# Attention and MLP in one kernel: a new order for the first loads, group sums on TensorE for two batches, and an earlier table load

## The chip, the cores and the metric

One core of a Trainium2 chip runs the whole kernel. The metric is the device time in microseconds (us). Each kernel is run several times, in rounds together with the kernel before on the same chip, and one run is recorded by the hardware profiler. Every run has a state, fast or slow, as judged by its time against the fastest run of the same kernel. A median that is quoted is of all runs.

Terms used throughout: TensorE (PE in the profile) multiplies matrices; PEld is its weight load; DVE is VectorE, ACT is ScalarE, POOL is GpSimd, SP issues transfers. A batch is one of the 8 attention batches. A group is 512 tokens of the MLP: nine groups, 0 to 8. "mm1" is the first MLP matmul of a group with its silu, "mm2" is the second. In the program, the attention of batch g+1 is interleaved with mm2 of group g.

## The reference, cut to what matters

```python
def _attn_ref(q, k, v):                   # q, k, v: [8, 8, 576, 64] float32
    q_d, k_d, v_d = mean of 4 neighbouring rows of q, k, v      # 144 rows
    out_d = softmax(q_d k_d^T / 8) v_d                          # coarse attention
    out_up = np.repeat(out_d, 4, axis=2)
    # local attention: only keys with |i - j| < 4
    out_local = softmax(masked q k^T / 8) v
    return out_up + out_local
# then x = the result as [4608, 512];  h = x @ w_in [512, 2048]
# g = h * sigmoid(1.702 h);  out = g @ w_out [2048, 512]
```

## The kernel before: the parts that matter

The prologue loads q/k, v and the weights, and computes attention of batch 0. v is loaded twice: once as rows for the local part (`load_v`, cast by `prep_v` to `vb`), once with four rows side by side (`load_v4`), from which `prep_v4` adds up the four-row sums (`vd`).

```python
    for qd in range(NQ):
        load_qk(0, qd)                     # gpsimd queue
    constants()                            # masks, identity, ones columns
    prep_qk(0, 0); pool_qk(0, 0)           # DVE transposes, POOL sums of four
    load_v(0, gate=lambda t: nc.vector.memset(t, 0.0))   # SP queue, 10 transfers
    load_v4(0)                                           # SP queue, 6 transfers
    load_w_in(0)
    prep_qk(0, 1); pool_qk(0, 1)
    # ... rest of w_in, q/k of batch 1, w_out
    steps = attention(0)
    # ... scores; prep_v(0), prep_v4(0) on DVE; load_v(1), load_v4(1); value part
    for g in range(n_groups):
        b = g + 1
        if b < B:
            # ... loads of q/k for b+1; transposes and sums for b;
            #     v and four-row v of b+1 cast and summed, those of b+2 loaded
        gT = mm1(g)
        steps = dict(zip(POS, attention(b))) if b < B else {}   # POS = [0, 18, 25, 32, 43, 52]
        mm2(g, gT, steps)                  # steps[n]() runs before matmul n of 64
```

The six steps of `attention` are: scores of the first half, scores of the second half, value part of two head pairs, of two more, transposes of two, of two more. They are hundreds of tiny matmuls:

```python
    def av(b, hp):                         # value part of one head pair: 44 matmuls
        o = ps_tile("av")
        for i in range(5):
            for par in range(2):
                for j in range(2):
                    # ...
                    nc.tensor.matmul(o[...], lhsT=E[...], rhs=vb[...], ...)     # es
        # ... 24 more for the coarse part, lhsT=Ed[...] (ed)
```

At the end of mm2 the table of ScalarE is switched back to silu:

```python
            nc.scalar.activation(out=osb, in_=ops, func=AF.Copy, scale=1.0 / GELU_SCALE)
            # ... store osb
        nc.scalar.preload_act_table_set("silu_and_others")
```

The softmax here doesn't subtract the row's maximum and nothing guards it: scores larger than these inputs give would overflow.

## Time and profile before

The median was 382.2 us (381.81 to 382.93, three runs). The profiled run has a span of 381.2 us.

The page cuts the span in 40 slices; each digit is the busy share in tenths, PEclk the clock granted to TensorE.

```profile
PE   0200369397799889988978899799999998999995
PEclk9999999789999999999999999999999999999999
DMA  7999999999769314961595149410010011002002
```

TensorE starves in the first five slices and is busy after that. The DMA engines are full while it starves (digits 7 to 9).

The chain of waits (start, length, what) gives the reason at the start:

```profile
8.54 0.73 SPq L129
...
17.57 11.85 DMA vf<-in_v_dram
29.60 1.51 DVE vb_86 L200
```

v of batch 0 is issued from 8.5 us and lands at 29.4 us. The four-row sums end later still, at 43.4 us, and steady mm1 matmuls run only from 53.9 us.

The windows view gives busy times by stage. I cut it at the first mm1 weight load of each group. The columns are the stretch, its length, busy time and number of instructions for each engine, the mean granted clock, the DMA share and the GB/s.

```profile
core 0: us, PE busy (x) PEld busy (x) DVE busy (x) ACT busy (x) POOL busy (x), PEclk, DMA share, GB/s
52.10:98.90 46.80, 36.12 (x620) 18.01 (x624) 18.72 (x27) 21.05 (x32) 26.34 (x26) 0.93 1.10 196
98.90:139.00 40.10, 35.09 (x618) 17.47 (x624) 14.22 (x25) 20.80 (x32) 17.34 (x19) 0.96 0.63 139
139.00:175.60 36.60, 33.47 (x619) 17.26 (x625) 15.02 (x26) 20.79 (x32) 17.34 (x19) 1.00 0.59 131
175.60:213.60 38.00, 33.25 (x619) 17.10 (x625) 14.96 (x26) 20.90 (x32) 17.34 (x19) 1.00 0.60 126
213.60:249.80 36.20, 32.94 (x618) 16.97 (x624) 14.88 (x25) 20.79 (x32) 17.35 (x19) 1.00 0.57 133
249.80:284.40 34.60, 32.84 (x618) 16.93 (x624) 14.87 (x25) 20.79 (x32) 15.23 (x15) 1.00 0.09 33
```

Rows are groups 0 to 5. Group 0 is stretched by waits for batch 1's data. Groups 1 to 4 take 36.2 to 40.1 us; group 5 takes 34.6 us.

A group boundary, ScalarE's timeline and the TensorE matmul that follows (start, length, engine, line, what; in brackets the idle time before it and what ended it):

```profile
139.43 0.60 ACT L445 ACTIVATE osb<-ops 128x512 f32<-128x512 f32 x1 [1.66 <-PE ops L438]
140.05 1.28 ACT L450 ACT_TABLE_LOAD   x1
141.34 1.09 ACT L424 ACTIVATE gT<-hps 128x512 bf16<-128x512 f32 x2
...
141.99 0.38 PE L418 MATMUL hps<-xT_82,w_in_bf 128*128 128x512 bf16 x1 [0.87 <-ACT gT L424]
```

The table load (1.28 us, begun 20 ns after the copy ends) stands between the last output copy and the first silu, and TensorE waits 0.87 us for that silu at each of the eight boundaries.

And a piece of the weight-load timeline in group 2:

```profile
163.33 1.19 PEld L438 LDWEIGHTS <-gT 128*128 128x128 bf16 x7
164.94 0.11 PEld L280 LDWEIGHTS <-es_92 64*64 64x64 bf16 x4 [0.42 <-DVE rc L306]
166.53 0.21 PEld L280 LDWEIGHTS <-es_92 64*64 64x64 bf16 x16 [1.48 <-issue]
```

TensorE stops after 4 of 20 weight loads of one tile, for 1.48 us, and the profile names no releaser ("issue").

### The profile page before, as it was taken

What the parts mean: (1) busy time and instruction counts of PE and PEld (TensorE: products, weight loads), DVE (VectorE), ACT (ScalarE), POOL (GpSimd) and SP (SyncE); (2) the same over time, 40 slices, a digit from 0 to 9 for tenths busy, and PEclk for the clock granted to TensorE, in tenths of its full rate; (3) what the DMA queues carried; (4) which work ended last, traced back from release to release, by engine and by line L of the source; (5) the groups of instructions that cost most, each with busy time, mean ns of one, the idle gap of its engine ahead of it and who ended that gap; (6) DMA issues with size and microseconds to landing.
All of it is one profiled execution on the core that took longest, in us unless ns stands there. A gap on an engine that the chain in (4) does not pass through costs nothing.

```text
span 381.2 us, 11310 instructions
## 1 busy us (share of the span) xinstructions
PE 302.0 (79%) x5065; PEld 153.9 (40%) x5120; DVE 133.2 (35%) x213; ACT 181.4 (48%) x278; POOL 140.8 (37%) x166
## 2 busy tenths in 40 slices
PE   0200369397799889988978899799999998999995
PEld 0200234244344444544444445444544454444442
DVE  6602681226600670157015702660473063000000
ACT  1400056432466266726661666267547726624622
POOL 7932004894593029504940494069007000000000
PEclk9999999789999999999999999999999999999999
DMA  7999999999769314961595149410010011002002
GB/s 124 176 199 237 209 210 189 187 186 189 204 147 197 103 56 91 215 142 55 122 195 132 57 107 223 125 51 2 31 58 28 3 58 57 0 29 83 0 29 83
DMA packets 66289, 43.73 MB, mean 115 GB/s; under 512 B 44224, under 2 KB 57536, under 8 KB 66240
## 3 DMA queue, kind: packets, MB, share of 16 engines
q1 hardware_dynamic: 57408, 29.37, 34.3%
q0 software_dynamic: 8832, 13.63, 20.0%
q8 instruction: 40, 0.66, 0.7%
q14 instruction: 9, 0.07, 0.1%
HBM read 47.19 MB, written 9.44 MB: 149 GB/s over the span
## 4 chain that ended last, share of the span: by engine, by line
PE 64%; SPq 11%; DMA 11%; ACT 5%; issue 5%; POOL 3%; DVE 1%; ACTq 0%; DVEq 0%; POOLq 0%
PE ops L438 29%; PE hps L418 26%; SPq L129 11%; DMA vf<-in_v_dram 5%; DMA out_dram<-osb 3%; ACT L450 3%; DMA v_96<-in_v_dram 2%; PE sd L243 2%; PE av L280 2%; PE av L294 1%; PE xt L322 1%; ACT osb L445 1%; DMA qb_101<-in_q_dram 1%; ACT gT L424 1%; POOL vb_86 L200 1%
## 5 line engine op out<-in xcount | busy, mean ns | idle before, releaser
L438 PE MATMUL ops<-w_out_bf,gT 128*128 128x512 bf16 x532 | 125.2, 382 | 6.8 <-issue 6.3
L424 ACT ACTIVATE gT<-hps 128x512 bf16<-128x512 f32 x144 | 85.1, 597 | 39.2 <-PE hps L418 39.1
L418 PEld LDWEIGHTS <-w_in_bf 128*128 128x128 bf16 x576 | 56.8, 99 | 80.3 <-issue 15.3
L438 PEld LDWEIGHTS <-gT 128*128 128x128 bf16 x576 | 53.2, 98 | 62.7 <-issue 3.4
L418 PE MATMUL hps<-xT_82,w_in_bf 128*128 128x512 bf16 x143 | 54.9, 384 | 8.2 <-ACT gT L424 7.0
L418 PE MATMUL hps<-xT_85,w_in_bf 128*128 128x512 bf16 x144 | 55.2, 383 | 0.9 <-DVE xT_85 L366 0.4
L418 PE MATMUL hps<-xT_83,w_in_bf 128*128 128x512 bf16 x143 | 55.2, 386 | 0.3 <-issue 0.3
L445 ACT ACTIVATE osb<-ops 128x512 f32<-128x512 f32 x36 | 21.5, 597 | 69.7 <-PE ops L438 48.0
L418 PE MATMUL hps<-xT_84,w_in_bf 128*128 128x512 bf16 x135 | 52.0, 385 | 0.1
L344 ACT COPY od<-xt 128x576 f32<-128x576 f32 x32 | 19.1, 642 | 63.9 <-PE xt L333 63.0
L268 DVE TENSOR_TENSOR es_90<-es_90,mask 128x600 bf16<-128x600 bf16 x8 | 6.7, 842 | 96.4 <-ACT es_90 L254 96.4
L308 DVE TENSOR_TENSOR y<-av,rc 128x896 bf16<-128x896 f32 x32 | 34.9, 1092 | 1.1
L200 POOL CAST vb_87<-vf 128x2560 bf16<-128x2560 f32 x4 | 9.3, 2321 | 23.8 <-DMA v_96<-in_v_dram 23.8
L268 DVE TENSOR_TENSOR es_92<-es_92,mask 128x600 bf16<-128x600 bf16 x8 | 4.7, 589 | 30.2 <-ACT es_92 L254 30.2
L294 PE MATMUL av<-vd_88,ed_94 48*64 48x65 bf16 x192 | 4.0, 207 | 11.6 <-DVE vd_88 L209 11.3
L322 PE MATMUL xt<-ident,y 60*64 60x57 bf16 (+1 forms) x640 | 10.3, 198 | 3.5 <-DVE y L308 1.9
L306 DVE RECIPROCAL rc<-av 128x14 f32<-128x14 f32 x32 | 7.7, 240 | 14.9 <-PE av L294 14.9
L280 PE MATMUL av<-vb_86,es_90 64*64 64x65 bf16 x80 | 1.5, 209 | 14.3 <-DVE vb_86 L200 14.3
L322 PEld LDWEIGHTS <-y 60*64 60x64 bf16 x640 | 8.1, 112 | 10.1 <-DVE y L308 4.8
L450 ACT ACT_TABLE_LOAD x9 | 11.5, 1283 | 0.2
L294 PEld LDWEIGHTS <-ed_94 48*64 48x64 bf16 x384 | 5.5, 111 | 14.4 <-issue 14.4
L378 ACT ACT_TABLE_LOAD x8 | 10.3, 1283 | 0.9 <-PEq L522 0.8
(318 smaller groups left out, 365.5 us busy)
## 6 DMA issues: line engine op xcount, KB each, us to landing
vf<-in_v_dram SPq DMA_DIRECT2D x80, 128.0 KB, 3.8
v_96<-in_v_dram SPq DMA_DIRECT2D x48, 192.0 KB, 6.3
out_dram<-osb SPq DMA_DIRECT2D x36, 256.0 KB, 2.0
w_in_bf<-in_moe_w_in_dram POOLq DMA_DIRECT2D x4, 512.0 KB, 9.1
w_out_bf<-in_moe_w_out_dram POOLq DMA_DIRECT2D x4, 512.0 KB, 21.6
kb_99<-in_k_dram POOLq DMA_DIRECT2D x1, 288.0 KB, 4.5
qb_101<-in_q_dram POOLq DMA_DIRECT2D x1, 288.0 KB, 5.2
kb_103<-in_k_dram POOLq DMA_DIRECT2D x1, 288.0 KB, 6.1
```

The source lines that it names most:

```text
L129: nc.sync.dma_start(out=t[64 * par : 64 * par + 64, i], in_=bass.AP(tensor=v.tensor, offset=v[b, 0].offset + (114 * i + KSTART[par]) * D, ...
L200: eng.tensor_copy(out=vbs[b % 2][:, :, :, 0:D], in_=vf[b])
L268: nc.vector.tensor_tensor(out=ev, in0=ev, in1=mask, op=ALU.mult)
L294: nc.tensor.matmul(o[64 * pos : 64 * pos + 64, j, c0 : c0 + 65], lhsT=Ed[64 * j : 64 * j + 48, u, q0 : q0 + 64], rhs=vd[64 * j : 64 * j + ...
L308: nc.vector.tensor_tensor(out=y, in0=ov[:, :, :, 0:D], in1=rc.to_broadcast([128, 2, 7, D]), op=ALU.mult,)
L322: nc.tensor.matmul(x[64 * j : 64 * j + 64, par, 57 * i + c0 : 57 * i + c1], lhsT=y[64 * pos : 64 * pos + 60, par, i, :], rhs=ident[64 * po ...
L344: nc.scalar.copy(out=od.rearrange("p (x t f) -> p x t f", x=2, f=4), in_=x[:, :, 288:360, None].to_broadcast([128, 2, 72, 4]),)
L418: nc.tensor.matmul(hps, lhsT=w_in_bf[:, dmc, ffc * 128 : (ffc + 1) * 128], rhs=xT[dmc][:, tok0 : tok0 + TG], start=(dmc == 0), stop=(dmc = ...
L424: nc.scalar.activation(out=gT[:, ffc, :], in_=hps, func=AF.Silu, scale=GELU_SCALE)
L438: nc.tensor.matmul(ops, lhsT=gT[:, ffc, t * 128 : (t + 1) * 128], rhs=w_out_bf[:, ffc, :], start=(ffc == 0), stop=(ffc == n_ffc - 1),)
L445: nc.scalar.activation(out=osb, in_=ops, func=AF.Copy, scale=1.0 / GELU_SCALE)
L450: nc.scalar.preload_act_table_set("silu_and_others")
```

## The change

The intent has three parts. First, the startup: v of batch 0 gets the DMA engines nearly to itself, w_in, w_out and q/k of batch 1 follow in the order in which they are needed, and later v loads come one batch ahead rather than two. Second, the four-row loads of batches 0 and 1 are dropped; TensorE makes these sums from `vb` with a selection matrix `psel`, which needs more constants. For batch 1 the attention comes late in mm2 of group 0, its value part after all of it. Third, the silu table is loaded right after the last exp of a group. The core of the diff (constants cut):

```diff
+    def prep_vd_pe(b):
+        vb, vd = vbs[b % 2], vds[b % 2]
+        p = ps_tile("vdp")
+        pv = p.rearrange("p x n -> p (x n)")
+        for kc, iis in ((0, (0, 1)), (1, (1, 2, 3)), (2, (3, 4))):
+            for i in iis:
+                for j in range(2):
+                    nc.tensor.matmul(
+                        pv[64 * j : 64 * j + 64, 256 * kc : 256 * kc + 256],
+                        lhsT=psel[:, i, kc, :],
+                        rhs=vb[:, i, :, :].rearrange(
+                            "p (hp j) d -> p hp j d", j=2)[:, :, j, 0:D],
+                        start=(i == iis[0]), stop=(i == iis[-1]),
+                        tile_position=(0, 64 * j))
+        nc.scalar.copy(out=vd[:, :, :, 0:D], in_=...)
@@ attention, second scores step
             exp_down(1, st["d", 1])
+            nc.scalar.preload_act_table_set("silu_and_others")
             mask_local(1)
@@ end of mm2
-        nc.scalar.preload_act_table_set("silu_and_others")
@@
     POS = [0, 18, 25, 32, 43, 52]
+    POS0 = [36, 52, 64, 64, 64, 64]
@@ prologue
     load_v(0, gate=lambda t: nc.vector.memset(t, 0.0))
-    load_v4(0)
-    load_w_in(0)
     prep_qk(0, 1)
     pool_qk(0, 1)
-    for c in range(1, 4):
-        load_w_in(c)
-    for qd in range(NQ):
-        load_qk(1, qd)
+    load_w_in(0, 512)
+    load_w_in(512, 512)
+    load_w_in(1024, 1024)
     for c in range(4):
         load_w_out(c)
+    for qd in range(NQ):
+        load_qk(1, qd)
@@
     prep_v(0, nc.vector)
-    prep_v4(0, nc.vector)
-    load_v(1)
-    load_v4(1)
+    prep_vd_pe(0)
@@ group loop, g > 0 (cut)
             prep_qk(b, 0)
             pool_qk(b, 0)
+            prep_v(b, nc.gpsimd)
             if b + 1 < B:
-                prep_v(b + 1, nc.gpsimd)
-                if b + 2 < B:
-                    load_v(b + 2)
+                load_v(b + 1)
             prep_qk(b, 1)
             pool_qk(b, 1)
+            prep_v4(b, nc.gpsimd)
             if b + 1 < B:
-                prep_v4(b + 1, nc.gpsimd)
-                if b + 2 < B:
-                    load_v4(b + 2)
+                load_v4(b + 1)
```

In group 0, mm2 also takes its matmuls in another order, so that w_out is used as it arrives, and the v loads of batch 2 come after it.

## The prediction

> **What bounds it now.** The windows view cuts the 381.2 us into stages. From the second group on TensorE is the limit: 28.7 to 38.8 us per group, TensorE busy for 86 to 96%. Before that it starves: busy 9.6 of the first 52.1 us; the TensorE timeline has steady w_in matmuls only from 53.9 us. The chain of waits names v loads: those of batch 0 are issued from 8.5 us and land at 29.4, sharing saturated DMA queues (about 200 GB/s from 15 us on) with the four-row v loads, 2 MB of w_in, qk of batch 1 and w_out. The four-row sums end at 43.4 us, and attention of batch 0 needs 10 us more. Group 0 is stretched too: after mm1 (68 us) TensorE waits until 75.9 us for qdT, since POOL stood at batch 1's v until 62.6 us. mm1 of group 1 starts at 99.1 us, in earnest at 103.2. Each group boundary has a 0.87 us gap (8 gaps, 7.0 us, waits view): osb, 1.28 us table load, silu.
>
> **Removed, added, moved.**
> 1. The four-row loads of batches 0 and 1 go (1.15 MB each) with their adds (DVE 3.4 us, POOL 6.0 us). Instead: 14 matmuls of 256 columns and an ACT copy of 128x768, by estimate 1.5 to 3 us and 0.85 us (from the 216 ns pitch of 512-column matmuls and the 0.64 us copy of 576 columns).
> 2. v of batch 0 competes with almost nothing; in steady state ten such loads take about 10.5 us.
> 3. Cost: POOL makes 1,920 columns of iota (estimate 3 us; its 2,560-column cast takes 2.3), then some ten DVE ops. [...]the first transpose slips from 5.9 to about 9.3 us, the v gate from 8.4 to about 12. v lands near 22.5, vd is ready near 28, steady mm1 starts near 37.5 us: 16 us gained.
> 4. w_in (from 19 us), w_out, qk of batch 1 follow at about 0.18 MB/us: in by 34, 45 and 52 us, just in time.
> 5. Group 0: the value part of attention 1 comes after all of mm2, exposed: about 12 us. But the 8 us wait and the slow start of group 1 go. mm1 of group 1 starts near 79.5 us.
> 6. Silu load off the boundary: 7 gaps, about 6 us.[...]
> 7. Later v comes one batch ahead, not two. POOL work per batch is about 16 us from the start of mm1, needed about 20 us in: hidden.
>
> **Sum.** mm1 of group 1 about 22 us earlier, 2 us less cold clock, 6 us less gaps: 352 us, 80% range 343 to 361. Chances: faster by over 2% 0.96, within 2% 0.03, slower 0.01.
>
> **Right if:** first transpose at 9 to 10 us; v of batch 0 landed by 24; steady mm1 from 34 to 41; mm1 of group 1 at 75 to 84 with no 8 us wait for qdT; a hole of 8 to 12 us after mm2 of group 0; no TensorE wait for gT at boundaries; groups 2 to 6 at 34 to 37 us.
>
> **Wrong if:** waits for w_in or w_out in group 0, the DMA queue being slower than thought; batch 1's v landing after 66 us (its gate stands behind qk of batch 1); late v or four-row v in group 1 (slack about 4 us); unexplained issue gaps of 1.2 to 1.7 us on TensorE, which come and go.

The sum is 382.2 - 22 - 2 - 6 = 352 us, and the table load of 1.28 us and its 0.87 us gap are read from the trace of the kernel before.

## The result, and the profile after

The changed kernel took 367.56 us (median of four runs, 364.92 to 371.92, one of them slow) against 382.0 us. Ratios in this document are the mean time of one kernel's fast runs over the mean of the kernel before's fast runs of the same rounds, so not quite the ratio of the quoted medians: here 0.9598, 95% interval 0.9524 to 0.9672. It is faster, but 15.6 us slower than predicted and outside the range of 343 to 361 us. The profiled run has a span of 367.2 us.

The same slices of the page, after:

```profile
PE   0224899959978999699969997999999999999996
PEclk9998699977998999699989999899999999999999
DMA  7499975998894149712991099317710011002002
```

TensorE reaches a busy share of 80% in the fifth slice, where before it did so in the seventh. But its clock drops six times. Before, the trace's clock records have two drops ahead of the very end, at 72.4 us for 6.8 us and at 103.1 us for 3.4 us, the second too short to show in a slice.

The start, by the chain of waits:

```profile
18.41 5.81 DMA vf<-in_v_dram
24.40 1.51 DVE vb_86 L224
25.95 1.72 PE vdp L246 x14
27.69 0.81 ACT vd_88 L255
...
35.38 2.39 issue
```

v is cast from 24.4 us, the sums by TensorE took 1.72 us and their copy 0.81 us. This part went as predicted, apart from the last line: an "issue" gap of 2.39 us within attention 0 (what it is comes below).

The windows by group (0 to 5) after:

```profile
38.30:81.60 43.30, 37.89 (x647) 19.12 (x638) 18.01 (x26) 21.56 (x34) 13.65 (x17) 0.89 0.92 176
81.60:124.40 42.80, 38.11 (x634) 17.99 (x626) 16.77 (x29) 21.30 (x33) 17.34 (x19) 0.89 0.74 144
124.40:163.70 39.30, 36.18 (x625) 17.94 (x624) 15.07 (x25) 20.90 (x32) 17.34 (x19) 0.91 0.58 122
163.70:202.50 38.80, 35.48 (x625) 17.43 (x624) 15.17 (x26) 20.90 (x32) 17.35 (x19) 0.96 0.59 123
202.50:240.80 38.30, 35.53 (x626) 17.54 (x625) 15.07 (x26) 20.90 (x32) 17.33 (x19) 0.96 0.64 126
240.80:274.40 33.60, 33.60 (x626) 16.98 (x625) 14.97 (x26) 20.90 (x32) 15.23 (x15) 1.00 0.47 108
```

mm1 of group 1 starts at 81.6 us, not 98.9: 17.3 us gained. Then groups 1 to 4 take 42.8, 39.3, 38.8 and 38.3 us, in sum 159.2 us, against 150.9 us before: 8.3 us lost again. Groups 5 to 8 take 126.4 us, against 131.4: 5.0 us gained. The sum is 17.3 - 8.3 + 5.0 = 14.0 us, the difference of the spans. So the question is why groups 1 to 4 grew, and only they.

A boundary after (ScalarE's timeline) shows that the third part works; the silu follows the output copy without a table load, and TensorE waits at no boundary:

```profile
164.16 0.60 ACT L500 ACTIVATE osb<-ops 128x512 f32<-128x512 f32 x1 [1.66 <-PE ops L492]
165.02 0.60 ACT L471 ACTIVATE gT<-hps 128x512 bf16<-128x512 f32 x1 [0.27 <-PE hps L465]
```

The weight-load timeline in group 2, after:

```profile
147.06 0.15 PEld L340 LDWEIGHTS <-ed_94 48*64 48x64 bf16 x7
150.44 0.34 PEld L340 LDWEIGHTS <-ed_94 48*64 48x64 bf16 x17 [3.23 <-issue]
150.85 0.13 PEld L492 LDWEIGHTS <-gT 128*128 128x128 bf16 x2
151.25 0.15 PEld L492 LDWEIGHTS <-gT 128*128 128x128 bf16 x1 [0.28 <-issue]
```

The gap is now 3.23 us, in another place, and after it the loads of mm2 come 0.43 us apart (in the lines that follow these): twice the usual 0.216 us. The clock has been halved: the trace's clock records have 0.5 from 149.3 us for 6.8 us. Nearly the same gap is in groups 1, 3 and 4 (by starts of weight loads 3.46, 3.54 and 2.99 us, and 3.33 us here).

### What the gaps are

The trace records every weight load of TensorE, 5,148 of them, so a gap can be placed in the program: each matmul is two instructions, a weight load and the matmul. In the changed kernel the four long gaps come before instructions 3003, 4281, 5559 and 6837 of TensorE's stream. The remainders by 256 are 187, 185, 183 and 181. In the kernel before, the "issue" gaps of groups 1 to 4 come before 2749, 4281, 5303, 5559 and 6837; remainders 189, 185, 183, 183, 181. The remainder slips by two with each group, because this count leaves out what else the trace records on TensorE: 21 instructions, two of them semaphore waits in each group with attention. Counted with these, all the gaps just named stand at remainder 194 (the first of before at 195), and so do 81 gaps of over 1.2 us in the 14 traces: 68 at 194, 13 at 195. The gaps stand at steps of 256 instructions. The two "issue" gaps of attention 0 in the changed kernel, 1.72 us and 2.39 us, are among them (before instructions 703 and 959).

The trace has a DMA queue of the kind "instruction", q8. This is the DMA view of the stretch of the gap above (queue, kind: packets, MB, share of 16 engines):

```profile
q0 software_dynamic: 232, 0.48, 81.6%
q1 hardware_dynamic: 221, 0.23, 26.7%
q8 instruction: 1, 0.02, 1.9%
```

In the 3.1 us of the gap the engines move 453 packets of data and one packet of instructions. Over the run the queue moves 40 packets of 16,384 bytes, 0.66 MB; TensorE's stream of 10,296 weight loads and matmuls, with the 21 others, is 40.3 times 256. So I take q8 to bring TensorE's instructions, one packet for each 256. And in every gap of over 2.5 us at these places, in all 14 traces, TensorE goes on 2.2 to 2.6 us after an instruction packet has started.

So the theory, called F below, which is inferred from these counts and times: when TensorE passes from one block of 256 to the next, the block after that is fetched, and the fetch must come in before these 256 are used up. Where mm1 and mm2 run without attention a block lasts some 28 us (27.7 us from 320.9 us in the changed kernel), in an attention burst 3 us (the table's 2.98). The table gives, for group 2, the time from the block change to the end of the gap, and the time for which the block's instructions lasted:

| kernel | block change, us | instruction packet starts, us | first instruction of the next block, us | change to next | instructions lasted | gap |
|---|---|---|---|---|---|---|
| before (4281) | 160.34 | 164.22 | 166.53 | 6.20 | 4.62 | 1.58 |
| after (4281) | 144.13 | 148.11 | 150.44 | 6.31 | 2.98 | 3.33 |

(The block change is read where the weight load executes; the request itself is not in the trace and may come a little sooner.) The fetch takes as long in both. But the block in the kernel before held 14 matmuls of mm2 with 256 instructions in 4.6 us, and the block after held 7 of them and lasted 3.0 us. The change had moved the block borders: it put 2 x 14 matmuls, 56 instructions, into the stream before group 1.

The rival theory, called D: the change moved the loads. v comes one batch ahead, and these loads now collide with the attention, whatever the stream. A further one: the moved table load has to do with it. And: the gaps are chance.

### The profile page after: what moved, and what is told of

It reads as the page before. It is cut to its first block, busy times and chain, and to the rows that moved or that the text cites. A ratio compares the mean times of both kernels' runs of the same rounds, so it can differ in the third digit from the quotient of the medians.

```text
span 367.2 us, 11384 instructions
## 1 busy us (share of the span) xinstructions
PE 315.8 (86%) x5148; PEld 157.5 (43%) x5148; DVE 130.3 (35%) x219; ACT 180.8 (49%) x278; POOL 134.1 (37%) x157
## 4 chain that ended last, share of the span: by engine, by line
PE 82%; issue 6%; DVE 5%; ACT 2%; SPq 2%; DMA 2%; POOL 1%; DVEq 0%; POOLq 0%; ACTq 0%
PE ops L492 36%; PE hps L465 34%; PE av L340 2%; PE av L326 2%; DVE y L354 2%; SPq L153 2%; PE xt L368 2%; PE sd L289 2%; DMA vf<-in_v_dram 2%; PE xt L379 1%; PE vdp L246 0%; DVE xT_84 L406 0%; DVE vb_86 L224 0%; ACT osb L500 0%; DVE xT_85 L406 0%
## 5 line engine op out<-in xcount | busy, mean ns | idle before, releaser
L492 PE MATMUL ops<-w_out_bf,gT 128*128 128x512 bf16 x576 | 137.7, 393 | 0.0
L471 ACT ACTIVATE gT<-hps 128x512 bf16<-128x512 f32 x144 | 86.0, 597 | 44.7 <-PE hps L465 44.7
L492 PEld LDWEIGHTS <-gT 128*128 128x128 bf16 x576 | 54.6, 100 | 65.4 <-issue 7.0
L465 PE MATMUL hps<-xT_84,w_in_bf 128*128 128x512 bf16 x144 | 55.7, 387 | 0.9 <-DVE xT_84 L412 0.9
L465 PE MATMUL hps<-xT_85,w_in_bf 128*128 128x512 bf16 x144 | 55.7, 387 | 0.5 <-DVE xT_85 L412 0.5
L465 PE MATMUL hps<-xT_82,w_in_bf 128*128 128x512 bf16 x144 | 56.1, 390 | 0.0
L465 PE MATMUL hps<-xT_83,w_in_bf 128*128 128x512 bf16 x144 | 56.0, 389 | 0.0
L390 ACT COPY od<-xt 128x576 f32<-128x576 f32 x32 | 19.1, 641 | 42.8 <-PE xt L379 42.8
L314 DVE TENSOR_TENSOR es_90<-es_90,mask 128x600 bf16<-128x600 bf16 x8 | 4.3, 536 | 89.8 <-ACT es_90 L300 89.8
L354 DVE TENSOR_TENSOR y<-av,rc 128x896 bf16<-128x896 f32 x32 | 34.9, 1092 | 1.1
L314 DVE TENSOR_TENSOR es_92<-es_92,mask 128x600 bf16<-128x600 bf16 x8 | 4.2, 531 | 25.1 <-ACT es_92 L300 25.1
L379 PE MATMUL xt<-ident,y 36*64 36x36 bf16 x256 | 8.1, 188 | 3.3 <-issue 3.3
L273 PE MATMUL sl_194<-qT_146,kT_144 32*64 32x60 bf16 x40 | 0.9, 242 | 11.6 <-DVE vf L517 11.6
L406 DVE TENSOR_TENSOR xT_82<-xt,od 128x570 bf16<-128x570 f32 x8 | 6.0, 752 | 9.8 <-ACT od L390 9.8
```

Of the source, the lines that this page charges most:

```text
L314: nc.vector.tensor_tensor(out=ev, in0=ev, in1=mask, op=ALU.mult)
L354: nc.vector.tensor_tensor(out=y, in0=ov[:, :, :, 0:D], in1=rc.to_broadcast([128, 2, 7, D]), op=ALU.mult,)
L379: nc.tensor.matmul(x[64 * j : 64 * j + 64, xx, 288 + 36 * c2 : 324 + 36 * c2], lhsT=y[64 * pos : 64 * pos + 36, j, 5 + c2, :], rhs=ident[6 ...
L390: nc.scalar.copy(out=od.rearrange("p (x t f) -> p x t f", x=2, f=4), in_=x[:, :, 288:360, None].to_broadcast([128, 2, 72, 4]),)
L465: nc.tensor.matmul(hps, lhsT=w_in_bf[:, dmc, ffc * 128 : (ffc + 1) * 128], rhs=xT[dmc][:, tok0 : tok0 + TG], start=(dmc == 0), stop=(dmc = ...
L471: nc.scalar.activation(out=gT[:, ffc, :], in_=hps, func=AF.Silu, scale=GELU_SCALE)
```

## The experiments

Twelve kernels were run, in four jobs on different chips; each is compared with the kernel before of its own job by the ratio. "Gap" below is the time between the starts of two successive weight loads.

| kernel | median us | ratio to before (95% interval) | groups 1 to 4, us |
|---|---|---|---|
| before | 382.2 | 1 | 40.1, 36.6, 38.0, 36.2 |
| after | 367.56 | 0.9598 (0.9524 to 0.9672) | 42.8, 39.3, 38.8, 38.3 |
| e1_pad200 | 363.79 | 0.9489 (0.9431 to 0.9546) | 41.2, 36.2, 35.5, 34.8 |
| e2_before_pad56 | 388.71 | 1.0174 (1.0124 to 1.0224) | 39.0, 38.1, 39.8, 36.4 |
| e3_no_late_loads | 350.99 | 0.9164 (0.9119 to 0.9210) | 36.8, 34.7, 34.4, 33.6 |
| e4_silu_late | 373.91 | 0.9781 (0.9736 to 0.9826) | 40.6, 37.9, 39.5, 37.6 |
| e5_control | 369.38 | 0.9633 (0.9568 to 0.9697) | 42.6, 40.0, 38.8, 36.9 |
| e6_gated | 360.16 | 0.9393 (0.9322 to 0.9463) | 37.3, 34.8, 34.9, 34.1 |
| e7_overlap | 369.45 | 0.9598 (0.9508 to 0.9688) | 39.5, 39.0, 40.1, 37.0 |
| e8_both | 357.71 | 0.9310 (0.9225 to 0.9395) | 36.1, 37.3, 34.8, 35.0 |
| e9_spread | 353.10 | 0.9219 (0.9173 to 0.9265) | 41.0, 33.7, 34.5, 33.6 |
| e10_keep_v4 | 374.20 | 0.9776 (0.9714 to 0.9839) | 41.3, 37.7, 37.8, 35.4 |
| e11_gated_pad200 | 365.36 | 0.9552 (0.9503 to 0.9602) | 37.7, 35.7, 37.2, 39.8 |
| e12_spread2 | 347.09 | 0.9101 (0.9044 to 0.9157) | 34.5, 34.8, 34.7, 33.6 |

All gave the right result but e3_no_late_loads. The medians are of all runs, with one slow run each in after, e1_pad200, e7_overlap and e8_both. The groups come from one profile of each kernel. The profile of e7_overlap is of a slow run.

### e1_pad200: move the block borders back

```diff
         load_qk(0, qd)
+    padt = consts.tile([128, 64], BF16, name="padt")
+    nc.vector.memset(padt, 0.0)
+    pad = psM.tile([128, 512], FP32, name="pad", tag="psM")
+    for _ in range(100):
+        nc.tensor.matmul(pad[0:32, 0:32], lhsT=padt[:, 0:32], rhs=padt[:, 32:64],
+                         start=True, stop=True)
     constants()
```

> The changed kernel with 200 more TensorE instructions (100 tiny matmuls of zeros into an unread tile) while TensorE waits for the first loads. Theory F (instruction fetch): the 56 instructions that the change added to TensorE's stream (2 x 14 matmuls, each with its weight load) moved the 256-instruction blocks against the attention bursts; with 56 + 200 = 256 the blocks stand as before the change, the stalls of 3 to 3.5 us in groups 1 to 4 shrink to below 2.4 us and no longer drop the clock: half-clock time in those groups from 17 us to under 5, groups 1 to 4 about 10 us less in sum, total about 355 us (352 to 359). Rival D (the moved loads alone, v one batch ahead, collide with the attention): unchanged, 365 to 368 us, stalls of 3 us stay.

More instructions made the kernel faster: 363.79 us, ratio 0.9489 against 0.9598 (and 0.9633 in the repeat). In the total this is little (the interval just touches that of after, not that of the repeat); the groups show it better. In group 2 the gap stands after 4 weight loads of the same tile as in the kernel before (weight-load timeline):

```profile
151.89 0.11 PEld L326 LDWEIGHTS <-es 64*64 64x64 bf16 x4 [0.42 <-DVE rc L352]
154.02 0.21 PEld L326 LDWEIGHTS <-es 64*64 64x64 bf16 x16 [2.02 <-issue]
```

Groups 1 to 4 take 147.7 us, 11.5 us less than after; the expectation said about 10. Gaps in groups 2 to 4 are 2.13, 1.52 and 1.29 us, and the clock stays full there. The size of the total was missed. Group 0 took 46.6 us, 3.3 more, as the padding moved the borders there too (gaps of 1.89 and 1.78 us), and group 1 kept a gap of 2.94 us and 9.8 us at half clock: 3.4 us after this gap, and 6.4 us of a spell that began in the exposed attention before it. D had no reason for any of this in groups 2 to 4: the loads are where they were. And those groups are in sum 106.5 us, where the kernel before has 110.8, of which 2.6 us are its three boundary gaps. So in these profiles nothing of the loss in groups 2 to 4 is left for the moved loads.

### e2_before_pad56: move the borders in the kernel before

The edit is the same loop, 28 times in place of 100, in the kernel before.

> The kernel before with only 56 more TensorE instructions (28 tiny matmuls) in its idle start. Theory F: the blocks stand as in the changed kernel, stalls of about 3 us appear in groups 1 to 4 and drop the clock: 386 to 393 us. Rival D: unchanged, 382 us.

It took 388.71 us, ratio 1.0174. In group 2 the kernel before now stops where the changed kernel stops, after 7 loads of the same tile:

```profile
165.58 0.15 PEld L294 LDWEIGHTS <-ed 48*64 48x64 bf16 x7
169.03 0.23 PEld L294 LDWEIGHTS <-ed 48*64 48x64 bf16 x17 [3.30 <-issue]
```

The gaps come before instructions 3003, 4281, 5559 and 6837, the four of the changed kernel, with 2.97, 3.40, 3.30 and 1.62 us. So 56 instructions more, the only edit of this run, moved the gaps there. The size of the effect in the total is less clean: groups 1 to 4 grew from 150.9 to 153.3 us only (the 3.40 us gap did not drop the clock), and 2.8 us of the 5.6 us in this profile are a later start of mm1 (54.9 us), with v of batch 0 landing later. I had not expected that part, and one profile cannot tell it from scatter.

### e3_no_late_loads: take the other transfers away

```diff
                 for qd in range(NQ):
-                    load_qk(b + 1, qd)
+                    kf[b + 1, qd] = kf[b, qd]
+                    qf[b + 1, qd] = qf[b, qd]
@@
             if b + 1 < B:
-                load_v(b + 1)
+                vf[b + 1] = vf[b]
@@
-            if b + 1 < B:
-                load_v4(b + 1)
```

> The changed kernel without the q, k and v loads of batches 3 to 7 (it computes them from batch 2's data: a wrong result on purpose), all instructions on TensorE unchanged. Theory F says that a fetch takes 5 to 6 us from block change to first instruction only because other transfers hold the DMA engines: all long stalls in groups 1 to 4 vanish though the blocks stand as in the changed kernel, groups 2 to 4 take 33.6 to 34.5 us as the quiet groups 5 and 6 do, total about 345 us (343 to 350). If the stalls have to do with the stream alone, 365 us.

The same stream, the same place in group 2, but a short gap:

```profile
143.57 0.15 PEld L340 LDWEIGHTS <-ed 48*64 48x64 bf16 x7
144.57 0.23 PEld L340 LDWEIGHTS <-ed 48*64 48x64 bf16 x17 [0.85 <-issue]
```

From block change to the next block's first instruction it now takes 4.07 us where it took 6.31; the instructions last 3.12 us, about as long as in after. The difference lies ahead of the instruction packet: it starts 1.83 us after the block change, not 3.98, and from its start to the first instruction it takes 2.23 us, in after 2.33. Groups 2 to 4 take 34.7, 34.4 and 33.6 us, the first 0.2 us over the expected range. The total, 350.99 us, is 1 us over the expected range; mm1 of group 0 started 2.8 us later than in the profile of after. So in these runs a long gap took both: a border in a burst and other transfers in the way.

### e4_silu_late: undo the third part

```diff
             exp_down(1, st["d", 1])
-            nc.scalar.preload_act_table_set("silu_and_others")
             mask_local(1)
@@ end of mm2, and once before the group loop
+        nc.scalar.preload_act_table_set("silu_and_others")
```

> The changed kernel with the silu table load back at the end of mm2 (TensorE's stream unchanged). Both theories: each of 8 boundaries gets its gap of 0.9 us back, about 7 us slower than the changed kernel: 371 to 375 us. If the load's place was worth nothing: 366 us.

373.91 us, as expected: ratio 0.9781 against 0.9598 and 0.9633, so 1.5 to 1.8% of 382 us, 5.7 to 7.0 us. The long gaps stay before instructions 3003, 4281 and 5559 (3.09, 3.30 and 3.03 us): the table load has no part in them.

### e5_control: the changed kernel again

> The changed kernel itself once more, for a comparison on one chip with the next three: 365 to 368 us, and its stalls of 3 us and more again at the same places of TensorE's stream (instructions 3003, 4281, 5559, 6837). If the stalls were chance, they stand elsewhere.

369.38 us, 1.4 us over the expected range. The gaps come before 3003, 4281, 5559 and 6837 again, with 3.73, 3.95, 3.52 and 1.73 us (the last is split with one of 1.54 us before 7093). They are not chance. Their lengths vary by run, their places don't.

### e6_gated: move the loads out of the bursts

```diff
         elif b < B:
-            if b + 1 < B:
+            if g == 1:
                 for qd in range(NQ):
                     load_qk(b + 1, qd)
@@
-            if b + 1 < B:
-                load_v(b + 1)
@@
-            if b + 1 < B:
-                load_v4(b + 1)
@@ before mm2(g, gT, steps); a gate is a one-element memset by DVE
+        def late_v(b=b):
+            load_v(b + 1, gate=zero)
+            load_v4(b + 1)
+        def late_qk(b=b):
+            for qd in range(NQ):
+                load_qk(b + 2, qd, gate=zero)
+        if g > 0 and b + 1 < B:
+            steps.setdefault(33, []).append(late_v)
+        if g > 0 and b + 2 < B:
+            steps.setdefault(53, []).append(late_qk)
```

> The changed kernel with the v, four-row v and q/k loads of batches 3 to 7 begun only after the value part of each group's attention (all data and sums as before; right result). Theory F: during the attention bursts of groups 2 to 4 the DMA engines are nearly free, a fetch takes 2 to 3 us, no stall over 1.5 us and no half clock; groups 2 to 4 take 34 to 35.5 us (39.4, 38.8, 38.3 before), group 1 37 to 40; total 350 to 356 us. Rival: stalls that belong to the stream stay, 366 us. A loss is possible if the later loads come too late for the next batch.

All the data is loaded as before, v later within a group and q/k at the end of the group before. 360.16 us, 9.2 us less than e5_control of the same job. Groups 2 to 4 take 34.8, 34.9 and 34.1 us and group 1 37.3, all within what was expected; from block change to next in group 2 it takes 4.19 us (the expectation had 2 to 3 for a fetch), and the block lasted that long, so TensorE did not wait. The total missed its range (350 to 356), for a reason that had been named as possible: in group 5 the sums came too late (weight-load timeline):

```profile
247.76 0.14 PEld L342 LDWEIGHTS <-ed 48*64 48x64 bf16 x5
249.79 0.11 PEld L342 LDWEIGHTS <-ed 48*64 48x64 bf16 x4 [1.88 <-issue]
251.81 0.20 PEld L342 LDWEIGHTS <-ed 48*64 48x64 bf16 x15 [1.91 <-issue]
```

These gaps also read "issue", but they stand before instructions 7933 and 7941, away from the borders, and eight instructions apart; GpSimd wrote the three parts of these sums until 247.5, 249.7 and 251.8 us. The label alone doesn't tell a missing instruction from a missing operand: the place in the stream does.

### e7_overlap and e8_both: hide attention 1 in mm2 of group 0

```diff
-    POS0 = [36, 52, 64, 64, 64, 64]
+    POS0 = [8, 20, 32, 38, 46, 54]
@@
-                steps[64].insert(0, lambda: prep_vd_pe(1))
+                steps.setdefault(30, []).append(lambda: prep_vd_pe(1))
```

> The changed kernel with attention of batch 1 spread over mm2 of group 0 (steps 8, 20, 32, 38, 46, 54, sums by TensorE at step 30) in place of the end. The exposed tail of about 10 us and the half clock after it go if the data is there by then (v of batch 1 was cast at 60.1 us, step 30 comes near 63 us): mm1 of group 1 starts 6 to 10 us sooner, total about 359 us (356 to 363). If v or qk come too late or the fetches stall, 366 us.

A miss: 369.45 us against 369.38 of e5_control. The exposed tail went, but the profile has a gap of 3.68 us before instruction 1981 (remainder 189, a border) and 3.4 us at half clock after it: eight q/k loads had been issued at 62 to 66 us, just ahead of the gap at 73.9 us. Group 0 was no shorter (44.5 us against 43.0 in e5_control). This profile is of the slow run, but the fast one of e8_both shows the same.

e8_both has this edit and that of e6_gated.

> Both edits: if the two losses are independent, the gains add up: 341 to 349 us. If the earlier start of group 1 brings its attention nearer to the loads that feed it, less.

357.71 us, 2.5 us less than e6_gated (the intervals of the two ratios overlap), another miss, with the same gap in group 0 (3.92 us).

### e9_spread and e12_spread2: the same idea for the rest of the loads

e9_spread, against e8_both:

```diff
-            prep_v(1, nc.gpsimd)
             for qd in range(NQ):
                 load_qk(2, qd)
+            prep_v(1, nc.gpsimd)
         elif b < B:
-            if g == 1:
-                for qd in range(NQ):
-                    load_qk(b + 1, qd)
             prep_qk(b, 0)
             pool_qk(b, 0)
-            prep_v(b, nc.gpsimd)
             prep_qk(b, 1)
             pool_qk(b, 1)
+            prep_v(b, nc.gpsimd)
             prep_v4(b, nc.gpsimd)
@@
-        if g > 0 and b + 2 < B:
-            steps.setdefault(53, []).append(late_qk)
+        if b + 2 < B:
+            steps.setdefault(55 if g == 0 else 53, []).append(late_qk)
```

> The kernel of e8_both with three more moves of loads or of their users: q/k of batch 2 loaded before batch 1's v is cast, q/k of batch 3 only after attention 1 (in e8_both these eight loads were issued at 62 to 66 us, under the stall of 3.9 us in group 0), and in later groups the q/k sums before the v cast, so that the four-row sums end earlier (e6_gated waited 2 + 2 us for them in group 5). Theory F: stalls in group 0 below 2.5 us, group 0 about 40 us (45.4 in e8_both), groups 1 to 5 34 to 36 us: 347 to 353 us. If group 0 is limited by something else than fetches under loads, 355 to 358 us.

353.10 us, 0.1 us over the range. (The 62 to 66 us in the expectation are those of e7_overlap's trace; in e8_both the eight loads were issued from 59.8 to 64.1 us.) Group 0 takes 40.6 us (45.4 in e8_both) with no border gap over 1.0 us, groups 2 to 5 take 33.6 to 34.5 us. Group 1 waited 1.6 + 2.0 + 2.0 us for the sums of batch 2, which e12_spread2 loads sooner:

```diff
-        if g > 0 and b + 1 < B:
-            steps.setdefault(33, []).append(late_v)
+        if b + 1 < B:
+            steps.setdefault(39 if g == 0 else 33, []).append(late_v)
@@
-        if g == 0:
-            load_v(2)
-            load_v4(2)
```

> e9_spread with v and four-row v of batch 2 begun inside mm2 of group 0 (after the value part of attention 1) and not after its last output. In e9_spread group 1 waited 1.6 + 2.0 + 2.0 us for these sums, with 6.8 us of half clock after it (41.0 us; 33.6 to 34.5 in groups 2 to 6). With the loads 8 us sooner that wait goes: group 1 34 to 36 us, total 344 to 349 us. If the fetches in group 0 now meet these loads, the gain is given back there: 350 to 353 us.

347.09 us, as expected, 9% below the kernel before (ratio 0.9101; the changed kernel 0.9598). Slices of its page:

```profile
PE   0316599889999999899999999999999999999995
PEclk9999999999999999999999999999999999999999
```

No slice has a lowered clock. Groups 1 to 4 take 34.5, 34.8, 34.7 and 33.6 us, in sum 137.6 us where the changed kernel took 159.2. Its border gaps after mm1 of group 1 are 1.2 us at most.

### e10_keep_v4: without the sums by TensorE

```diff
     load_v(0, gate=lambda t: nc.vector.memset(t, 0.0))
+    load_v4(0)
@@
-    prep_vd_pe(0)
+    prep_v4(0, nc.vector)
@@ and the same for batch 1; the memset of v4 goes back to the constants
```

> The changed kernel with the four-row loads kept for batches 0 and 1 and summed by DVE and POOL (no sums by TensorE; new load order, late attention 1, and silu place kept). TensorE's stream has again the 10,242 instructions of before. If the start gained by the order of loads, v of batch 0 still lands near 24 us, but the four-row loads now run beside w_in: mm1 starts 6 to 9 us later than in the changed kernel (about 46 us). Groups 2 to 4 as in e1_pad200, 35 to 36 us each. Total 366 to 371 us. Rival D again has no reason for shorter groups 2 to 4: 374 us.

374.20 us, above the range. The start went as expected: mm1 at 45.2 us, 6.9 us later than in the profile of after, which is what the dropped four-row loads are worth there. Groups 2 to 4 take 110.9 us, between after (116.4) and e1_pad200 (106.5), though the borders stand as in e1_pad200. Group 0 took 46.0 us, with a border gap of 4.77 us. So with the borders moved back a part of the loss in groups 2 to 4 went here, not all that I had expected. The long gaps are at borders again, but the fetches took longer: from block change to next 6.9 and 7.1 us in groups 2 and 3 (gaps of 2.30 and 2.56 us, the second followed by 3.4 us at half clock), against 6.7 and 6.0 us in e1_pad200. Why they took longer was not looked into. D's number, 374 us, was hit, but not for its reason: it expected groups 2 to 4 unchanged.

### e11_gated_pad200: do the two edits add?

The edits are those of e6_gated and e1_pad200 together.

> e6_gated with the 200 further TensorE instructions of e1_pad200. Theory F: the two edits remove the same stalls, so little is left to gain: within 3 us of e6_gated (about 360 us) and not 5 us below it. If padding gained by something else (for instance a TensorE that was active early), the gains add: 354 to 356 us.

365.36 us, 0.9552 against 0.9393: slower than e6_gated, outside both expectations. In groups 1 to 4 the largest border gap is 1.26 us, so padding had nothing to gain there. It lost in group 0 (45.4 us against 43.9; gaps of 1.55, 2.57 and 1.57 us at moved borders, after two of 3.60 and 2.81 us in attention 0) and in late sums, which cost 2.0, 2.15 and 2.0 + 2.0 us in groups 2 to 4 and 10.2 us at half clock. Padding is a test, not a remedy.

## Why the prediction was wrong

Point by point:

1. Sums by TensorE: right. 1.72 us and 0.81 us measured, 1.5 to 3 and 0.85 predicted.
2. v with little competition: right in kind. It landed at 24.2 us, 22.5 predicted; w_in's loads ran beside its end.
3. Constants: right. The first transpose came at 9.2 us (9.3), the gate (the memset by DVE that holds v's loads back) at 11.5 (12). Steady mm1 came at 40.65 us, 37.5 predicted: the two border gaps of 1.72 and 2.39 us in attention 0 were not in the sum.
4. Weights just in time: right; TensorE waited for neither. w_in was in by 33.6 us, q/k of batch 1 by about 49.
5. Group 0: right. The value part of attention 1 is exposed, and mm1 of group 1 starts at 81.6 us, within 75 to 84.
6. Silu load: right; e4_silu_late puts it at 5.7 to 7.0 us, about 6 predicted.
7. "Later v comes one batch ahead, not two ... hidden": its conclusion, that the later groups keep their times, failed. The v loads were hidden; the groups still grew (groups 2 to 4 to 39.3, 38.8 and 38.3 us, where "34 to 37" stood).

The step that failed is in the sum. It took groups 1 to 4 as before, less the boundary gaps and "2 us less cold clock": 150.9 - 3.5 - 2 = 145.4 us. They took 159.2 us, 13.8 us more. The windows above split this. TensorE's busy time in these groups, which half clock stretches, was 145.3 us where 134.8 - 2 = 132.8 us was expected: 12.5 us more. Its idle time was 13.9 us where 16.1 - 3.5 = 12.6 us was expected: 1.3 us more, since the border gaps grew from 8.7 to 14.3 us in sum but other waits shrank. So it was above all the term "2 us less cold clock" that had the wrong sign: by the clock records, groups 1 to 4 had 3.4 us at half clock before and 23.3 us after.

A smaller term: "about 22 us earlier" was 17.3 us, 4.7 us missed (the prediction's own figures, 99.1 and 79.5 us, give 19.6). Groups 5 to 8 gained 1.5 us more than the 3.5 us of their four boundary gaps. And the prediction took 6 us for seven boundary gaps where the trace before has eight, 7.0 us. 13.8 + 4.7 - 1.5 - 1.0 = 16.0 us; the predicted span was about 351.2 us (381.2 - 30), the measured one 367.2.

The cause of most of this stands under "unexplained issue gaps ... which come and go" on the list of what could go wrong, at 1.2 to 1.7 us each. They do not come and go. As far as these runs show, they are waits for instructions: they stand at steps of 256 in TensorE's stream (remainder 194 or 195), in an attention burst, while data is loaded, and the change moved these borders by 56 instructions. From block change to first instruction it took 6.3 to 7.6 us under loads at the four long gaps after, and 3.7 to 4.1 us with nearly none at the three gaps of 0.8 to 1.0 us of e3_no_late_loads. Moving the borders back (e1_pad200) took away 11.5 of the 13.8 us. The rest is not shown to be theirs: of the 23.3 us at half clock, 17.0 follow the four long gaps, and 6.3 belong to a spell that began at 77.6 us in the exposed attention before group 1. Shown for the waits are the places (all kernels), the move of the gap with the count of instructions (e1_pad200 and e2_before_pad56, both ways), and its shortening without data transfers (e3_no_late_loads) or with transfers elsewhere in time (e6_gated, e12_spread2).

Through the clock the gaps cost more than their length. By the PEclk column of the windows, group 2 after ran (1 - 0.91) x 2 x 39.3 = 7 us at half clock (6.8 us by the clock records), before none. The half-clock spells within the runs are 3.4, 6.8, 10.2 or, once (e10_keep_v4), 13.7 us long. No length of a gap decided alone: one of 2.97 us (e2_before_pad56, group 1) was followed by a spell, and so were single gaps of 2.15 us (e11_gated_pad200, group 3) and 2.16 us (e8_both, group 2), while one of 3.40 us in e2_before_pad56 was not. What decides was not shown. The "issue" gaps of groups 1 to 4 before were 2.03 us or less, and none of them was followed by a spell (the one at 103.1 us there comes after waits for ScalarE); all four gaps of 2.99 to 3.54 us after were. That is why 1.6 us before and 3.3 us after differ by more than 1.7 us.

What stays open: when exactly a fetch is asked for, since the request is not in the trace; what the fetch waits for under loads before its packet starts (the packet itself took 0.96 us); how much of e2_before_pad56's 6 us belongs to the start; why the fetches of e10_keep_v4 took longer; why the landing of the same loads varies from run to run (with the same program up to there and on two chips, vb's cast, which waits for the ten v loads of batch 0, began at 22.3 us in e8_both and at 29.1 us in e9_spread); and what, beside the borders, made up the last 2.3 of the 13.8 us.

## What to carry to other kernels

A gap on TensorE in the middle of a run of small matmuls, with no releaser, is a question about its place in the stream: count instructions, the semaphore instructions too, take the remainder by 256 (the step of the 81 gaps in the 14 traces here), and look whether the kernel's other gaps share it. If so, keep large loads away from the bursts (here 9% off the kernel before where the change alone gave 4%), and expect that an edit which adds instructions ahead can move the gaps, as 200 did in e1_pad200 and 56 in e2_before_pad56. When a prediction lists "gaps that come and go", their sum over the kernel is part of the range.
